# Hedgehog attention and a gated causal convolution on one core: the first loads in another order, with a new list of steps

## The chip, the core and the metric

The kernel runs on one core of a Trainium2 chip. The core has five engines that run side by side, each through its own queue and in the order of that queue: PE (TensorE, matrix products), DVE (VectorE), ACT (ScalarE), POOL (GpSimd) and SP (SyncE). The last only starts transfers here and passes on semaphores. Transfers between the chip's memory and the core run on 16 DMA engines. They can be started from SP's queue, from ACT's queue and from POOL's queue. A transfer that changes the type on its way (float32 in memory, bfloat16 on the core) is started from POOL.

The metric is the device time of one execution in microseconds (us). The kernel before took 229.55 us (median of 3 runs, 228.45 to 229.55).

## The reference

There are 8 batches with 8 heads, 576 positions and head size 64. `q`, `k` and `v` come as float32. What is computed, cut to what matters:

```python
def phi(x):                                   # w_phi: 64 x 128
    proj = x @ w_phi
    proj = proj - max(abs(proj), axis=-1)
    return concatenate([exp(proj), exp(-proj)])
q_p, k_p = phi(q), phi(k)
kv = einsum('bhsf,bhsd->bhfd', k_p, v)
z = sum(k_p, axis=2)
num = einsum('bhsf,bhfd->bhsd', q_p, kv)
den = einsum('bhsf,bhf->bhs', q_p, z) + 1e-06
x = num / den                                 # to (batch, 576, 512)

gate = sigmoid(causal depthwise convolution of x with 5 taps)
out = (gate * (x @ w_val)) @ w_out
```

## The kernel before, in words

**Tiling.** The work is cut into 32 units, four for each batch. A unit is a pair of heads (`hp`, 0 to 3). Positions are split into 9 planes of 64. Planes 0 to 7 of a pair of heads make the unit itself. The ninth plane of all eight heads of a batch is gathered into one more piece per batch, whose steps carry an `e` at the end of the name. When the four units and the piece of a batch are through, the batch goes through convolution, `w_val` and `w_out`; the ninth planes of two batches share one last piece of that.

**The list of steps.** Everything after a short preamble is written out by hand in the string `ORDER`. A token such as `PQA3@0` is one step: its name, the unit or batch, after `@` the PSUM banks, after `:` the engine (A for ACT, D for DVE, P for POOL). A loop at the end of the kernel goes through the tokens inside `tc.manual_schedule()` and calls `op_<name>`. So each engine's queue holds its instructions in the order of the list, and no scheduler moves them. The steps that the texts below speak of:

- `LKa`, `LKb`, `LQa`, `LQb`: load heads 2 and 3, or heads 4 to 7, of batch 0's K or Q (`LKa0` is the second pair of heads, 128x576; `LKb0` the third and fourth, 128x2x576). `LK`, `LQ`, `LV`: all four pairs of a later batch. `LE`: the ninth plane of V. `LWV`, `LWO`: the two weights. All of these are started from POOL (line 288 for K and Q, 286 for V, 291 for `LE`, 321 and 330 for the weights). `LVa0` and `LVb0` load batch 0's V in float32 from SP, in two transfers each (line 286).
- The first pair of heads of batch 0 comes in float32 through two buffers named `QT` (line 195); `CK0` on DVE and `CQ0` on ACT turn it into bfloat16.
- `T`: eight transposes on PE, K first, then Q (line 344). `Tc`: the copy of the result out of PSUM. `PK`, `PQA`: projections of K and of Q (line 357). `mKa`, `mKb`, `mQ`: the row maxima on DVE (line 374). `Ka`, `Kb`: the exponentials of K on ACT, two instructions each (line 438). `E`: exponentials of the maxima (line 423).
- `DMQ`: on POOL, the maxima of Q spread over a diagonal, tile `DM` (line 409). `PQa`, `PQb`: the projection of Q in the other layout (line 527). `SH`: two products that subtract the maxima and read `DM` (line 543). `Qp`, `Qm`: the exponentials of Q on ACT (line 557).
- `V`: on POOL, V times the exponentials `E` (line 463, then a small cast). `DG0`: on POOL, the diagonal matrices of the convolution. `KV`, `KVM`, `NUM`, `RCP`, `XN`, `XP`, `XC`: the rest of the attention. `HL`, `GA`, `TH`, `VA`, `GV`, `OUT`, `OE`, `ST`: the convolution, the gate, `w_val`, `w_out` and the stores from SP (line 875).
- `FL`: a product of zeros on PE that nobody reads (line 253). There are 16 of them in the list, and 8 more in the preamble (line 226).

**Semaphores of the loads.** The loads that POOL starts signal their end through eight semaphores, `DMASW0` to `DMASW7`, which the program uses in turn. The ninth load uses the first one's semaphore again, and for that POOL waits, before it starts the ninth, until the first has landed; the tenth waits for the second, and so on.

**The preamble before.** It stands outside the hand-written order:

```python
    for name, eng in (("k", nc.sync), ("q", nc.scalar)):
        ...
        eng.dma_start(first[name], src[name][0, :, 0, :])
    wtmp = const.tile([P, F], FP32, name="wtmp")
    nc.sync.dma_start(wtmp[0:D, :], w_phi[:, :])
    nc.scalar.dma_start(wtmp[D:P, :], w_phi[:, :])
```

In the built program ACT starts the half of `w_phi` first and Q after it.

Of the kernel before, what the change touches and what calls it, by code (L numbers as in the profile page):

```python
# [33 lines left out]
WQ4 PQb4 SH4 Qm4 Qp4 Tc3:D PQA3@0 Tc5:D mKa2 LWV0 LV1 FL2@3 Ve0:P FL12@3 KV0@7 DMQ2:P DMQe0:P LE1 E2 FL7@3
PK3@3,2 KVM0:A Ka3 mQ3 DMQ3:P mKb3 KV1@4 KVM1:D mKa3 V2:P NUM0@0 Kb3 RCP0 FL15@4 XN0 T7@6 E3 Tc7:D WC0:A WC1:A
PQa2@4 WQ2 PQb2 SH2 PQa3@0 PQA5@2 WQ3 Qp2 mQ5 PQb3 XP0@6 T6@7 Tc6:D SH3 LWO0 NUM1@2 RCP1 XN1 Qm2 V3:P LQ2
XC0:D Qp3 KV2@4 PQea0@2 WQe0 PK5@5,7 mKb5 PQeb0 SHe0 Qm3 PQA6@0 mQ6 FL6@6 KVM2:A Qe0 V4:P KV3@4 NUM2@2 XP1@6
KVM3:D RCP2 XN2 Ka5 FL5@0 XC1:A Kb5 NUM3@0 WC2:A mKa5 NUMe0@3 WC3:A E5 XP2@6 PK6@4,2 RCPe0 XNe0 XPe0@3 Ve1:P
KV4@7 KVM4:A RCP3 XN3 XP3@5 PQa5@0 WQ5 XCe0:D XC2:D NUM4@6 XC3:D LWO1 mKa6 DMQ5:P RCP4 XN4 PQb5 HL0:P Kb6 SH5
VA0_0@3 Ka6 Qm5 Qp5 GA0@6,4 mKb6 V5:P KV5@2 KVM5:D T9@0 NUM5@1 Tc9:D THy0 PK7@4,5 RCP5 LWO2 E6 THx0 VA0_2@0  # L40
XN5 LV2 XP4@1 Ka7 XC4:A GV0_0 DMQe1:P PQa6@6 DMQ6:P GV0_2 mKa7 Kb7 T8@2 Tc8:D mKb7 WQ6 PQb6 PQea1@0 WQe1 SH6
Qm6 Qp6 V6:P LWO3 E7 PQeb1 PQA7@3 mQ7 SHe1 Qe1 LE2 VA0_1@2 GV0_1 KV6@5 KVM6:D PK8@7,6 mKa8 Te2@3 Kb8 DMQ7:P
# [942 lines left out]
```

## Time and profile before

| | before |
|---|---|
| median of the runs | 229.55 us |
| the profiled execution's own time | 229.49 us |
| its span, from the first to the last recorded instruction | 227.6 us |
| mean granted TensorE clock | 0.974 of full speed |
| busy: PE, DVE, ACT, POOL | 206.7, 187.1, 195.8, 164.1 us |
| waits of POOL for ACT's `E` (step `V`), for DVE's maxima (step `DMQ`) | 13.9 us, 11.9 us |

The profile is one execution. Its own time is 1.9 us above its span, which is what lies outside the recorded instructions. Busy times of matmuls include modelled ends, so a PE that is busy all the time is not PE at its peak. In rows of the timeline the first number is the start, the second the time covered, both in us; a bracket at the end gives the idle time of the engine before the row and what ended it. In rows of transfers the last number is the median time from the start of the issue to the landing. Where a row stands for several instructions that run into each other, the time is that of all.

### The profile page before, as it was taken

The page shows a single profiled execution, that of the slowest core. Times are in us where ns is not written, and L with a number is a line of the kernel's source. Part 1 is how long each engine was busy: PE and PEld are TensorE (multiplying, and loading weights), DVE is VectorE, ACT ScalarE, POOL GpSimd, SP SyncE. Part 2 cuts the span into 40 slices and gives each one's busy share as a digit, 9 for nine tenths or more (in the row PEclk, how much of TensorE's full clock was granted, in tenths as well). Part 3 has the DMA queues.
Part 4 walks back from the last instruction along what each step waited for, and adds up shares of the span by engine and source line. Part 5 has one row for each costly group of instructions (what it writes and reads, how often), then busy time and mean ns, then how long its engine had stood idle before and what let it go on. Part 6 is the DMA issues. An engine that isn't in the chain of part 4 may idle for free.

```text
span 227.6 us, 9113 instructions
## 1 busy us (share of the span) xinstructions
PE 206.7 (91%) x3884; PEld 135.6 (60%) x3884; DVE 187.1 (82%) x336; ACT 195.8 (86%) x389; POOL 164.1 (72%) x199
## 2 busy tenths in 40 slices
...
ACT  4439899999999989999999999999999999985350
POOL 7339999799989967994979874989983595851000
...
GB/s 139 212 180 105 209 136 45 114 39 115 70 143 107 167 240 95 16 177 128 119 116 97 127 96 68 128 170 189 176 106 3 6 80 111 95 49 3 141 131 145
DMA packets 27842, 26.12 MB, mean 115 GB/s; under 512 B 5653, under 2 KB 22933, under 8 KB 27802
## 3 DMA queue, kind: packets, MB, share of 16 engines
...
## 4 chain that ended last, share of the span: by engine, by line
PE 62%; DVE 15%; ACT 13%; issue 4%; DMA 3%; POOL 1%; ACTq 0%; DVEq 0%; POOLq 0%
PE PS L811 11%; PE PS L840 10%; PE PS L357 6%; ACT KT L438 5%; PE PS L575 5%; PE PS L485 5%; PE PS L776 5%; PE PS L344 4%; ACT QT L557 4%; DVE XN L595 3%; PE PS L527 3%; DMA QT<-in_q_dram 3%; DVE MK L374 2%; DVE MQ L374 2%; PE PS L605 2%
## 5 line engine op out<-in xcount | busy, mean ns | idle before, releaser
L438 ACT ACTIVATE KT<-PS 128x512 bf16<-128x512 f32 x128 | 68.7, 623 | 5.8 <-PE PS L357 4.7
L463 POOL TENSOR_TENSOR VT<-vN,E 128x1024 bf16<-128x1024 bf16 x28 | 53.3, 1905 | 15.0 <-ACT E L423 13.9
L557 ACT ACTIVATE QT<-PS 128x1024 bf16<-128x1024 f32 x64 | 63.1, 1054 | 0.8 <-PE PS L543 0.6
L374 DVE TENSOR_REDUCE MK<-PS 128x4 f32<-128x512 f32 x64 | 43.0, 683 | 2.1 <-PE PS L357 1.8
L374 DVE TENSOR_REDUCE MQ<-PS 128x8 bf16<-128x1024 f32 x32 | 39.0, 1220 | 6.8 <-PE PS L357 6.0
L409 POOL TENSOR_TENSOR DM<-id,MQ 128x512 bf16<-128x512 bf16 x32 | 33.3, 1039 | 12.5 <-DVE MQ L374 11.9
L840 PE MATMUL PS<-WOUT,GV 128*128 128x512 bf16 x128 | 32.2, 380 | 1.4 <-issue 1.4
L811 PE MATMUL PS<-XT,WVAL 128*128 128x512 bf16 x128 | 31.8, 380 | 0.1
L357 PE MATMUL PS<-W,T 64*128 64x128 bf16 x512 | 25.1, 221 | 5.5 <-ACT KTe L678 2.2
L357 PEld LDWEIGHTS <-T 64*128 64x128 bf16 x512 | 17.7, 96 | 13.2 <-issue 5.8
L485 PE MATMUL PS<-VT,KT 128*128 128x65 bf16 x512 | 24.5, 194 | 0.6 <-ACT QT L557 0.5
L485 PEld LDWEIGHTS <-KT 128*128 128x128 bf16 x512 | 21.8, 98 | 4.0 <-issue 0.8
L832 DVE SCALAR_TENSOR_TENSOR GV<-GATE,PS 128x512 bf16<-128x512 bf16 x32 | 20.9, 681 | 3.2 <-ACT GATE L800 1.6
L595 DVE TENSOR_TENSOR XN<-PS,RCP 128x512 bf16<-128x512 f32 x32 | 22.1, 692 | 1.3 <-DVE RCP L590 0.2
L150 DVE COPY T<-PS 128x1024 bf16<-128x1024 bf16 x29 | 19.6, 683 | 2.7 <-PE PS L344 2.6
L575 PEld LDWEIGHTS <-QT 128*128 128x128 bf16 x512 | 18.6, 97 | 4.9 <-issue 1.3
L489 PE MATMUL PS<-VZ,KTe 128*128 128x65 bf16 x128 | 21.3, 192 | 0.0
L575 PE MATMUL PS<-KVS,QT 128*128 128x65 bf16 x512 | 20.8, 193 | 0.3
L463 POOL TENSOR_TENSOR VZ<-vE,Ee 64x512 bf16<-64x512 bf16 x16 | 16.7, 1042 | 4.3 <-ACT Ee L423 3.7
L800 ACT ACTIVATE GATE<-PS 128x1024 bf16<-128x1024 f32 x16 | 15.8, 1037 | 3.7 <-PE PS L776 3.7
L527 PE MATMUL PS<-T,W 64*128 64x256 bf16 x128 | 18.6, 284 | 0.3
L840 PEld LDWEIGHTS <-GV 128*128 128x128 bf16 x128 | 11.0, 97 | 12.5 <-issue 2.3
...
## 6 DMA issues: line engine op xcount, KB each, us to landing
out_dram<-OS SPq DMA_DIRECT2D x28, 256.0 KB, 3.3
qN<-in_q_dram POOLq DMA_DIRECT2D x7, 576.0 KB, 6.1
kN<-in_k_dram POOLq DMA_DIRECT2D x7, 576.0 KB, 7.4
vN<-in_v_dram POOLq DMA_DIRECT2D x14, 256.0 KB, 6.4
OS<-in_v_dram SPq DMA_DIRECT2D x4, 256.0 KB, 7.7
...
```

The lines of the kernel that those rows point to most:

```text
L357: (nc.tensor.matmul(PS[:, banks[g], jj * F:(jj + 1) * F], T[row(g), n, jj, :, :].rearrange("p a t -> p (a t)"), W2[row(g), :], start=True, ...
L374: nc.vector.tensor_reduce(dst, x, AX.X, ALU.max, apply_absolute_value=True)
L409: engines[eng].tensor_tensor(u.DM[:, :, :], id64[:, :].unsqueeze(1).to_broadcast([P, n, 64]), u.MQ[:, :, :].rearrange("p j g -> p (j g)"). ...
L438: nc.scalar.activation(u.KT[:, ft, par, :, :].rearrange("p b f -> p (b f)"), PS[:, u.PK[par], :], AF.Exp, scale=1.0 if ft == 0 else -1.0,)
L463: engines[eng].tensor_tensor(dst[:, :, :, 0:D], x.unsqueeze(1).to_broadcast([rows, 2, n, D]), e.unsqueeze(3).to_broadcast([rows, 2, n, D]) ...
L485: nc.tensor.matmul(o, u.KT[:, ft, y % 2, h2 * 2 + y // 2, :], u.VT[:, ft, h2 * 4 + y, :], start=(y == 0), stop=False,)
L527: return nc.tensor.matmul(PS[:, u.PQ + a, :].rearrange("p (j g t) -> p g j t", g=2, t=64)[:, g, :, :], W2[row(g), :], u.T[row(g), 1, :, a, :],
L557: nc.scalar.activation(u.QT[:, ft, :, :, :].rearrange("p a n t -> p a (n t)"), half(u.PQ, 512), AF.Exp, scale=1.0 if ft == 0 else -1.0,)
L575: (nc.tensor.matmul(u.NUM[:, jj // 2, x * E1:(x + 1) * E1], u.QT[:, ft, jj // 2, 4 * h2 + 2 * (jj % 2):4 * h2 + 2 * (jj % 2) + 2, :].rearr ...
L595: nc.vector.tensor_tensor(u.XN[:, :, :, :], numview(u)[:, :, :, 0:D], u.RCP[:, :, :].unsqueeze(3).to_broadcast([P, 2, 4, D]), ALU.mult,)
L811: nc.tensor.matmul(PS[:, m.val[r], :], WVAL[:, dt, r, :], xt(b)[:, dt, 4:12, :].rearrange("p n t -> p (n t)"), start=(dt == 0), stop=(dt = ...
L840: nc.tensor.matmul(PS[:, m.out[j], :], m.GV[:, r, j * P:(j + 1) * P], WOUT[:, r, :], start=(r == 0), stop=(r == 3),)
```

## The change

**The preamble.** The first five transfers are now written inside `tc.manual_schedule()`. Their order on each queue is the written one: SP starts K, the first half of `w_phi` and the taps, as before; ACT now starts Q first and the second half of `w_phi` after it.

**The list.** `ORDER` is a new list with the same 1241 steps. All loads of batch 0's K and Q (`LQa0`, `LKa0`, `LQb0`, `LKb0`) stand ahead of batch 1's (`LQ1`, `LK1`). Both halves of batch 0's V stand ahead of the first `WQ` in SP's queue, where only `LVa0` did. Units now go 0, 1, 2, 3, 4 where they went 0, 1, 4, 2, 3. Steps change engines here and there: `HL` on ACT twice more (6 instead of 8 on POOL), `Tc` on ACT 5 instead of 3, `XC` on ACT 6 instead of 11, `XCe` on ACT 3 instead of 1, `Tce` on ACT none instead of one, `WC` on ACT 2 and POOL 2 instead of ACT 4, `KVM` on ACT 14 instead of 15, `OE` on ACT 20 instead of 19, `ND0` on POOL instead of DVE. The diff, with the list cut to its first two lines:

```diff
 ORDER = """
-ZV1:D ZV0:A IF0:D CK0 ZV2:D CQ0 T0@1 LKa0 LQ1 Tc0:A TP0@6 CW0 W0 PQA0@3 PK0@5,1 LQa0 FL8@0 FL1@7 FL11@6 LK1
-ND0:D mQ0 DG0:P FL10@0 Ka0 FL4@6 PQa0@6 mKb0 mKa0 E0 T1@2 FL3@0 Tc1:D PQA1@3 mQ1 PK1@0,5 T4@2 Kb1 Tc4:D mKb1
...
+LQa0 IF0:D ZV1:D CK0 ZV0:A CQ0 TP0@4 LKa0 T0@1 CW0 W0 T1@0 Tc0:D PK0@4,5 ZV2:D mKa0 PQA0@6 Tc1:A PK1@3,2
+FL12@1 LQb0 Kb0 mQ0 Ka0 PQA1@0 LKb0 LQ1 mKb1 mKb0 ND0:P Ka1 T2@6 Tc2:D E0 LK1 LE0 mQ1 LVa0 FL0@7 Te0@5 Tce0:D
...
     first = {}
-    for name, eng in (("k", nc.sync), ("q", nc.scalar)):
+    for name in ("k", "q"):
         t = featq.tile([P, 2, 2, 8, 64], BF16, name="QT")
         t = t[:, :, :, :, :].rearrange("p f h n t -> p (f h n t)").bitcast(FP32)
         first[name] = t[:, 0:NPL * D]
-        eng.dma_start(first[name], src[name][0, :, 0, :])
     wtmp = const.tile([P, F], FP32, name="wtmp")
-    nc.sync.dma_start(wtmp[0:D, :], w_phi[:, :])
-    nc.scalar.dma_start(wtmp[D:P, :], w_phi[:, :])
     cw5 = const.tile([5, DM], FP32, name="cw5")
-    nc.sync.dma_start(cw5[:, :], moe_conv_w[:, :])
+    with tc.manual_schedule():
+        nc.sync.dma_start(first["k"], src["k"][0, :, 0, :])
+        nc.scalar.dma_start(first["q"], src["q"][0, :, 0, :])
+        nc.sync.dma_start(wtmp[0:D, :], w_phi[:, :])
+        nc.scalar.dma_start(wtmp[D:P, :], w_phi[:, :])
+        nc.sync.dma_start(cw5[:, :], moe_conv_w[:, :])
```

The first place is POOL's queue in the opening, from the load of batch 1's Q on. Rows with `DMA` are loads; `kN`, `qN` and `vN` are the loaded K, Q and V, `GV` the buffer in which `w_val` lands, `WOUT` that of `w_out`, `DM` the spread maxima; the bracket names the semaphores that the instruction waits for. Before:

```order
L288 DMA qN<-in_q_dram 128x4x576
L288 DMA qN<-in_q_dram 128x576
L288 DMA kN<-in_k_dram 128x4x576
L270 TENSOR_TENSOR id_128<-ident 128x32 [waits Pool_49]
L271 TENSOR_TENSOR id_128<-id_128,ident 128x32 [waits Pool_49]
L272 TENSOR_TENSOR id_128<-id_128,ident 128x32 [waits Pool_49]
L273 TENSOR_TENSOR DIAG<-id_128,cwT 128x640 [waits DVE_49,Pool_49]
L288 DMA kN<-in_k_dram 128x2x576
L409 TENSOR_TENSOR DM<-id_126,MQ 128x512 [waits DVE_49]
```

And the change:

```order
L289 DMA qN<-in_q_dram 128x4x576
L251 TENSOR_TENSOR id_129<-ident 128x64 [waits Pool_49]
L289 DMA kN<-in_k_dram 128x4x576
L292 DMA vE<-in_v_dram 128x4x64 x2
L322 DMA GV<-in_moe_w_val_dram 128x4x512 [waits DMASW0_49]
L289 DMA qN<-in_q_dram 128x4x576 [waits DMASW1_49]
L287 DMA vN<-in_v_dram 64x8x256 [waits DMASW2_49]
L287 DMA vN<-in_v_dram 64x8x256 [waits DMASW3_49]
L289 DMA kN<-in_k_dram 128x4x576 [waits DMASW4_49]
L331 DMA WOUT<-in_moe_w_out_dram 32x4x512 [waits DMASW5_49]
L410 TENSOR_TENSOR DM<-id_129,MQ 128x512 [waits DVE_49,Pool_49]
```

Before, five loads were started ahead of the first `DM`, and the ninth load of POOL came 10 rows behind it. Now fourteen are started ahead of it (four more stand above the rows shown), and the last six wait for the first six: `DMASW4` is that of `LQ1`, `DMASW5` that of `LK1`. The three small sums of `DG0` have moved behind the second `DM`.

The second place is ACT's queue from the first conversion of Q (`qN<-QT`) to the first exponentials of Q (`QT<-PS`). `KT<-PS` are exponentials of K, two rows for a step, `KTe` those of the ninth planes. Before:

```order
L244 ACTIVATE qN<-QT 128x576
L148 ACTIVATE T<-PS 128x1024
L438 ACTIVATE KT<-PS 128x512 x2
L423 ACTIVATE E<-MK 128x8 x2
L438 ACTIVATE KT<-PS 128x512 x8
L557 ACTIVATE QT<-PS 128x1024
```

And the change:

```order
L245 ACTIVATE qN<-QT 128x576
L147 ACTIVATE T<-PS 128x1024
L439 ACTIVATE KT<-PS 128x512 x6
L424 ACTIVATE E<-MK 128x8 x2
L439 ACTIVATE KT<-PS 128x512 x4
L679 ACTIVATE KTe<-PS 128x512 x2
L439 ACTIVATE KT<-PS 128x512 x2
L558 ACTIVATE QT<-PS 128x1024 x2
```

Six steps of K (12 rows) and the ninth planes of K of batch 0 now stand ahead of the first exponential of Q, where five steps of K did.

More of the change, by code (lines that the diff above doesn't have):

```diff
@@ L28 @@
 ORDER = """
-ZV1:D ZV0:A IF0:D CK0 ZV2:D CQ0 T0@1 LKa0 LQ1 Tc0:A TP0@6 CW0 W0 PQA0@3 PK0@5,1 LQa0 FL8@0 FL1@7 FL11@6 LK1
-ND0:D mQ0 DG0:P FL10@0 Ka0 FL4@6 PQa0@6 mKb0 mKa0 E0 T1@2 FL3@0 Tc1:D PQA1@3 mQ1 PK1@0,5 T4@2 Kb1 Tc4:D mKb1
-LKb0 LVa0 PQA4@2 Kb0 Ka1 mQ4 PK4@4,5 Kb4 DMQ0:P LE0 WQ0 DMQ1:P PQb0 SH0 Qm0 LQb0 mKa1 Ka4 Te1@1 Tce1:D mKb4
-LK2 DMQ4:P PQa1@2 PKe1@0 mKe1 E1 WQ1 PQb1 SH1 Qp0 LVb0 FL13@5 FL0@5 FL9@5 Ee1 Qp1 V0:P FL14@5 Te0@5 mKa4 mQe1
-T2@6 Qm1 E4 KTe1 V1:P Tce0:D PKe0@4 Tc2:D mKe0 Ee0 PQA2@0 mQe0 mQ2 T3@3 T5@6 KTe0 PK2@2,7 Ka2 mKb2 Kb2 PQa4@4
@@ L34 @@
[L34 to L42, printed above, removed]
-XP5@2 XC5:D NUM6@4 RCP6 VA0_3@0 PQa7@1 WQ7 XN6 Tce2:A mKb8 Ka8 XP6@4 XC6:D E8 GV0_3 PQb7 SH7 PK9@6,3 Qp7 Qm7
@@ L99 @@
-OE7_0:A ST7_1 ST7_3 ST7_0
+LQa0 IF0:D ZV1:D CK0 ZV0:A CQ0 TP0@4 LKa0 T0@1 CW0 W0 T1@0 Tc0:D PK0@4,5 ZV2:D mKa0 PQA0@6 Tc1:A PK1@3,2
+FL12@1 LQb0 Kb0 mQ0 Ka0 PQA1@0 LKb0 LQ1 mKb1 mKb0 ND0:P Ka1 T2@6 Tc2:D E0 LK1 LE0 mQ1 LVa0 FL0@7 Te0@5 Tce0:D
+mKa1 LE1 Kb1 PK2@7,6 T3@4 Ka2 Tc3:D PKe0@0 mKa2 FL10@5 PQA2@2 mQ2 LVb0 LWV0 KTe0 PQa0@4 WQ0 LQ2 LV1 Kb2 PQb0
+LK2 LWO3 DMQ0:P SH0 FL4@7 mKb2 FL15@7 FL9@7 DMQ1:P DG0:P mKe0 PQa1@2 FL3@7 FL14@7 WQ1 PQb1 SH1 Qm0 Qp0 Ee0 Qp1
+T4@7 LWO1 DMQ2:P mQe0 DMQe0:P Qm1 Tc4:D Te1@6 Ve0:P FL5@4 Tce1:D PQA4@4 mQ4 PKe1@0 PQA3@6 mQ3 E1 PK4@2,3 E2
```

120 lines of the change are left out of this document (65 added, 55 removed).

## The prediction, on record before the change was run

> **What bounds the kernel now.** The page comes first, its busy times and its slices, then the busy times by stretch.
>
> ```profile
> PE 206.7 (91%) x3884; PEld 135.6 (60%) x3884; DVE 187.1 (82%) x336; ACT 195.8 (86%) x389; POOL 164.1 (72%) x199
> ACT  4439899999999989999999999999999999985350
> POOL 7339999799989967994979874989983595851000
> ```
>
> ```profile
> 0.00:10.00 10.00, 5.05 (x28) 2.51 (x30) 3.79 (x13) 4.26 (x5) 4.84 (x14) 0.88 0.83 166
> 10.00:20.00 10.00, 8.35 (x84) 4.22 (x80) 7.48 (x10) 5.70 (x13) 6.39 (x8) 0.67 0.88 142
> 20.00:30.00 10.00, 6.78 (x95) 3.95 (x94) 8.51 (x14) 9.35 (x23) 9.84 (x13) 0.94 1.18 202
> 30.00:40.00 10.00, 8.85 (x182) 6.75 (x179) 8.77 (x15) 10.00 (x21) 9.96 (x13) 1.00 0.66 76
> 60.00:80.00 20.00, 19.94 (x438) 13.05 (x438) 18.92 (x33) 19.35 (x38) 18.55 (x23) 1.00 0.92 141
> ```
>
> The columns of the second fence are the length, then busy PE, PEld, DVE, ACT and POOL, the granted clock, the DMA share and GB/s. From 60 to 80 us PE, ACT and DVE are all busy for 95% or more: no engine has room to win back lost time. What can be won or lost lies in the opening, where ACT is busy for 4.26 and 5.70 of 10 us, and in the tail. From 20 to 40 us POOL has nothing to spare either (9.84 and 9.96 of 10). So I follow ACT, and POOL when it feeds ACT. The timeline of ACT in the opening:
>
> ```profile
> 7.21 0.68 ACT L244 ACTIVATE qN<-QT 128x576 bf16<-128x576 f32 x1 [2.68 <-DMA QT<-in_q_dram]
> 8.59 1.02 ACT L148 ACTIVATE T<-PS 128x1024 bf16<-128x1024 bf16 x1 [0.70 <-PE PS L344]
> 10.74 1.08 ACT L438 ACTIVATE KT<-PS 128x512 bf16<-128x512 f32 x2 [1.12 <-PE PS L357]
> 12.78 0.31 ACT L423 ACTIVATE E<-MK 128x8 f32<-128x8 f32 x2 [0.95 <-DVE MK L374]
> 15.70 4.03 ACT L438 ACTIVATE KT<-PS 128x512 bf16<-128x512 f32 x8 [2.61 <-PE PS L357]
> 19.56 1.08 ACT L557 ACTIVATE QT<-PS 128x1024 bf16<-128x1024 f32 x1
> 21.62 1.09 ACT L557 ACTIVATE QT<-PS 128x1024 bf16<-128x1024 f32 x1
> 24.72 1.17 ACT L678 ACTIVATE KTe<-PS 128x512 bf16<-128x512 f32 x2
> 27.70 2.07 ACT L438 ACTIVATE KT<-PS 128x512 bf16<-128x512 f32 x4 [0.65 <-PE PS L357]
> ```
>
> ACT waits 2.68 us for Q, later 2.61 us for the second unit, whose inputs land late. From 15.70 us on it has one more gap, 0.65 us.
>
> **When the loads land.** The answers on the DMA issues, one by one, and the issues' own starts on POOL:
>
> ```profile
> kN<-in_k_dram POOLq DMA_DIRECT2D x1, 144.0 KB, 5.7
> qN<-in_q_dram POOLq DMA_DIRECT2D x1, 144.0 KB, 9.9
> kN<-in_k_dram POOLq DMA_DIRECT2D x1, 576.0 KB, 12.3
> kN<-in_k_dram POOLq DMA_DIRECT2D x1, 288.0 KB, 6.8
> OS<-in_v_dram SPq DMA_DIRECT2D x1, 256.0 KB, 9.7
> ```
>
> ```profile
> 1.28 0.75 POOL L288 DMA_DIRECT2D kN<-in_k_dram  x1 [0.34 <-issue]
> 2.36 1.33 POOL L288 DMA_DIRECT2D qN<-in_q_dram  x2
> 3.67 0.83 POOL L288 DMA_DIRECT2D kN<-in_k_dram  x1
> 10.64 0.76 POOL L288 DMA_DIRECT2D kN<-in_k_dram  x1
> ```
>
> POOL's loads land in the order of their issue: `LKa0` (144 KB) at 1.28 + 5.7 = 7.0 us; `LQ1` and `LQa0` (720 KB more) by about 3.1 + 9.9 = 13.0; `LK1` (576) at 3.67 + 12.3 = 16.0; `LKb0` (288) at 10.64 + 6.8 = 17.4. That is 720 KB in 6.0 us, 120 KB/us, up to 13.0, and 864 KB in 4.4 us, 196 KB/us, after it. The difference is what SP and ACT move meanwhile: the last of the first V pair lands at about 3 + 9.7 = 12.7 us, by when K, Q, the small ones and V make some 1160 KB, about 99 KB/us from 1 us on.
>
> **The change, part by part.** *Q first.* Q would be in by 4.5 to 6.5 us instead of 7.2; `ZV0` holds ACT until 4.5. But on PE unit 1's transposes now stand ahead of unit 0's projections, and they wait for `LKa0`, now second in POOL's queue: 7.0 + 144/120 = 8.2 us. So Q first costs nothing and wins nothing by itself; PE goes on at 8.2 us either way.
>
> *Batch 0 ahead of batch 1.* `LKb0` now ends 864 KB of POOL's queue, which by the row of `LQa0` is 13.0 us, where `LQb0` was issued only at 17.78 us. ACT's steps ahead of the first exponential of Q are six of K (four took 15.70 to 19.56, 0.97 each), E (0.31), KTe (0.98 up to the next row) and one copy (1.02). Started at about 9 us and held up for about 1 us by the third unit, they end at about 18.1 us. Taken alone, this part is a gain.
>
> *The wait on POOL.* `DMQ0`, which the first exponential of Q needs, now stands behind fourteen loads, and the fourteenth, `LWO3`, waits for `DMASW5`, that is until `LK1` has landed. Issuing alone would not hurt: fourteen at about 0.75 us from 1.28 us on end near 12.7. The landing does. Ahead of and with `LK1` stand 144+144+288+288+576+576 = 2016 KB. SP now has both halves of V at the start, 512 KB more, so at 99 KB/us its traffic lasts until 12.7 + 5.2 = 17.9 us. With 144 KB in at 7.0 and 120 KB/us until 17.9, 1452 KB are in; the other 564 at 196 take 2.9: `LK1` lands at 20.8 us. Bounds: 196 KB/us throughout gives 16.6, 120 throughout 22.6. I take 20.8, since both rates come from the same rows under the same kind of traffic.
>
> The Trainium skill, DMA: Bandwidth & Descriptors, section "Anatomy of one DMA — SWDGE (gpsimd) path", puts a transfer from this queue at about 2.0 us plus its bytes over 436 GB/s; as an estimate from that page all of the opening's traffic, about 3.8 MB, would be in near 12 us and `DMQ0` would wait for no load. The 12.3 us of the 576 KB row above disagree.
>
> Behind the wait, POOL runs `LWO3`, then `DMQ0`; PE adds `SH0`:
>
> ```profile
> 34.46 0.59 POOL L330 DMA_DIRECT2D WOUT<-in_moe_w_out_dram  x1
> 11.64 1.03 POOL L409 TENSOR_TENSOR DM<-id,MQ 128x512 bf16<-128x512 bf16 x1 [0.24 <-DVE MQ L374]
> 18.48 0.71 PE L543 MATMUL PS<-DM,minus 64*128 64x512 bf16 x2
> 10.64 2.31 PE L253 MATMUL PS<-zero 128*128 128x512 bf16 x5
> 8.00:12.00 4.00, 3.40 (x28) 2.10 (x29) 2.09 (x5) 2.11 (x3) 2.32 (x3) 0.50 1.18 238
> ```
>
> 20.8 + 0.59 + 1.03 + about 0.4 (the two products overlap) = 22.8 us for the first exponential of Q. By then ACT has done 1.02 + 5.8 + 0.31 + 0.98 = 8.1 us of work that counts; before, it had done that at 21.4 us (1.02 + 1.08 + 0.31 by 13.1, the remaining 5.7 from 15.70). **Term one: 22.8 - 21.4 = +1.4 us**, bounds 16.6 giving -2.8 (18.6 against 21.4) and 22.6 giving +3.2. Queued behind `DMQ0` on POOL are `DMQ1`, `DG0`, `DMQ2` and all of V; behind `SH0` on PE stand five fillers, unit 1's Q and then batch 1's first transposes. DVE and ACT wait for these.
>
> *After the wait.* PE will have stood still from about 16 us on. The last row shows what follows such a stand: after PE's idle time from 4.7 to 7.9 us the clock is 0.50, and five fillers take 2.31 us. Between `SH0` and `SH1` are five fillers and unit 1's products of Q, about 3.5 us cold; ACT has 2.0 us to do meanwhile (`Qm0`, `Qp0`, `Ee0`). That is 1.5 us lost cold and nothing warm; I take 1.0, nearer cold. On the other side, the gap of 0.65 us at 27.05 goes. **Term two: +0.35.** The first V is due on POOL at about 32.5 us instead of 22.2, since `Ve0` now stands ahead of it; batch 0's last V ends at about 41 us. Its product `KV3` ran at 39.8 us before and stands later in the new list, so I cost this at nothing more; if that cover is gone it is up to 1 us.
>
> *Steps on other engines.* By means of the page's groups: ACT gains two `HL` of about 1.0 (the POOL copy of that shape takes 1.02), two `Tc` of 1.05, one `OE` of 0.62 and two `XCe` of 0.45, and loses five `XC` of 0.61, two `WC` of 0.68, one `Tce` of 0.67 and one `KVM` of 0.43: **+0.2 us**. DVE comes to about the same (+0.1), PE does the same work.
>
> *The tail.*
>
> ```profile
> 217.51 3.71 PE L840 MATMUL PS<-WOUT,GV 128*128 128x512 bf16 x16
> 219.15 1.08 ACT L860 ACTIVATE OS<-PS 128x512 f32<-128x512 f32 x2 [1.70 <-PE PS L840]
> 219.78 4.95 SPq L875 DMA_DIRECT2D out_dram<-OS  x8
> ```
>
> The eight last stores run back to back from the first finished piece. Before, that piece is done after 6 of the last 16 products, now after 4, by the order of the `OUT7` steps: 2 x 0.22 = 0.43 earlier. **-0.4 us**, bounds -0.43 and 0, if the stores then wait for the last piece.
>
> **Sum** against the profiled execution's 229.49 us (span 227.6 and 1.9 outside; the median of the runs is 229.55): 229.49 + 1.4 + 0.35 + 0.2 - 0.4 = **231.0 us**. The new list's body from 45 us on is taken as neutral; before, the body has about 7 us of idle ACT between 40 and 200 us, so it could be a microsecond or two either way.
>
> **The rivals.** *The loads come sooner.* If `LK1` lands by 16.6 us, `SH0` no longer holds ACT, and the earlier inputs count in full: 229.49 - 2.8 - 0.65 + 0.2 - 0.4 = 225.8 us. For it: 196 KB/us was reached when POOL's queue was alone. Against it: SP moves 512 KB more at that very time. It decides once `LK1` lands before about 18. This is also where the page's rule would lead. Chance 0.20.
>
> *The loss is won back.* The first exponential of Q is late, but DVE and PE are not behind by as much (DVE has unit 3's copy and batch 0's ninth planes done by then), and the body's idle ACT takes it up: 229.49 + 0.2 - 0.4 = 229.3 us. For it: POOL waits 13.9 us for E over the run, so it can catch up. Against it: ACT's 19.35 of 20 us. Chance 0.22.
>
> *Slower still.* The 120 KB/us hold all the way, `LK1` lands at 22.6, PE stays cold for all five fillers, and V's delay reaches `KV3`: 231.0 + 1.8 + 0.5 + 0.7 = 234.0 us. It decides from a landing after about 22 us. Chance 0.12.
>
> *The preamble does nothing.* Q may land no sooner, since K and Q now start together on the same engines. With PE waiting for `LKa0` until 8.2 us, a Q at 6.5 changes no number above; it has no time of its own.
>
> **How the numbers follow.** The forecast, a late `DMQ0` at 231.0 us, own range 229.8 to 233.0, has 0.46. Half a per cent, 1.15 us around 229.55, is about what a measurement of this kernel can tell from no change: 228.40 to 230.70. Above it lies about 0.29 of the forecast's chance, the slower rival's 0.12 and 0.05 of the loss won back: slower 0.46. Within it lie the forecast's other 0.16 and 0.13: 0.29. Below it the first rival and 0.04: faster 0.25 with rounding. The range from 226.3 to 234.0 us leaves out about a tenth on each side at most. Cases of both signs hold most of the chance, so the forecast's own range stands beside it.
>
> **What would show it.** In the changed profile: POOL's row of `LWO3` starts when `LK1` lands, at 20 to 22 us, with no busy POOL between the issue of `LE1` and it but five loads; the first `DM` follows it; ACT's first QT row starts at 22 to 23.5 us with an idle time of 3 to 5 us put down to PE L544; the granted clock is near 0.5 to 0.7 from 16 to 26 us; the third unit's transposes come near 13 us, ahead of 22.8 before. I am wrong in the cause if `DM` stands at 12 to 18 us, and wrong in its worth if ACT is that late and the time is still at or below 229.

## The result, and the profile after

The changed kernel took 226.86 us (median of 7 runs, 225.52 to 227.71) beside 229.55 us for the kernel before (7 runs): a ratio of 0.988, 95% interval 0.984 to 0.991, some 2.8 us faster. The forecast was 231.0 us and slower; the time lies below its own range of 229.8 to 233.0 us, near the low end of the wide one (226.3 to 234.0). Taken again beside other kernels it came to 227.09 us, ratio 0.988 (0.984 to 0.993).

The profiled execution after took 225.52 us, span 223.6, the lowest of its runs. First the page: the engines' totals, and the slices of ACT and of the granted clock.

```profile
PE 202.7 (91%) x3848; PEld 134.1 (60%) x3884; DVE 186.1 (83%) x337; ACT 195.8 (88%) x387; POOL 163.7 (73%) x200
ACT  5591899999999999998999999999999999887640
PEclk9995899999999999999999999999999999999998
```

ACT's busy time is the same 195.8 us in a span 4.0 us shorter. The hole that the prediction spoke of is there: ACT has a slice with 1, and the granted clock is 5 in that slice and 8 in the next. The timeline of POOL after, where the wait stands:

```profile
16.28 0.76 POOL L289 DMA_DIRECT2D kN<-in_k_dram  x1 [3.76 <-DMA qN<-in_q_dram]
19.22 0.55 POOL L331 DMA_DIRECT2D WOUT<-in_moe_w_out_dram  x1 [2.18 <-DVE MQe L375]
19.79 2.04 POOL L410 TENSOR_TENSOR DM<-id,MQ 128x512 bf16<-128x512 bf16 x2
28.68 1.90 POOL L464 TENSOR_TENSOR VT<-OS,E 128x1024 bf16<-128x1024 f32 x1
```

`LK2` starts when `LQ1` has landed (16.3 us), `LWO3` when `LK1` has (19.2), and the first `DM` right behind it. The releaser that the second row names is an inference and wrong: the row's wait is for `LK1`'s semaphore by the order of the program. The last row is the first `V`. What ACT and PE make of it:

```profile
4.60 0.68 ACT L245 ACTIVATE qN<-QT 128x576 bf16<-128x576 f32 x1 [0.28 <-DMA QT<-in_q_dram]
8.14 1.02 ACT L147 ACTIVATE T<-PS 128x1024 bf16<-128x1024 bf16 x1 [2.85 <-PE PS L345]
21.54 1.94 ACT L558 ACTIVATE QT<-PS 128x1024 bf16<-128x1024 f32 x2 [4.57 <-PE PS L544]
24.67 1.94 ACT L558 ACTIVATE QT<-PS 128x1024 bf16<-128x1024 f32 x2 [1.00 <-PE PS L544]
```

```profile
20.89 0.61 PE L544 MATMUL PS<-DM,minus 64*128 64x512 bf16 x2 [4.60 <-POOL DM L410]
```

PE stands for 4.60 us and ACT for 4.57, then ACT once more for 1.00: the late `DMQ0` is as forecast. The second profile of the same kernel had it later still, close to the forecast's figures (`LWO3` was put at 20.8, the first exponential of Q at 22.8). POOL, then ACT, of that execution:

```profile
20.56 0.55 POOL L331 DMA_DIRECT2D WOUT<-in_moe_w_out_dram  x1 [2.04 <-DMA kN<-in_k_dram]
```

```profile
22.88 1.94 ACT L558 ACTIVATE QT<-PS 128x1024 bf16<-128x1024 f32 x2 [4.21 <-PE PS L544]
```

So the wait came as said and the time did not. The busy times by stretch from 95 us on say where to look. Columns: length, then busy PE, PEld, DVE, ACT, POOL, clock, DMA share, GB/s. Before:

```profile
95.00:160.00 65.00, 64.15 (x1276) 43.49 (x1277) 60.61 (x107) 62.45 (x126) 52.93 (x62) 1.00 0.75 126
160.00:210.00 50.00, 49.70 (x1048) 33.66 (x1045) 44.33 (x83) 46.43 (x92) 32.12 (x36) 1.00 0.34 69
```

And after (the page's first line shows that 36 of its matmul records are missing, so PE's own busy time reads a little low here):

```profile
95.00:160.00 65.00, 63.83 (x1257) 43.41 (x1263) 61.95 (x108) 62.32 (x127) 55.38 (x66) 1.00 0.70 112
160.00:210.00 50.00, 49.08 (x1076) 33.46 (x1085) 40.66 (x77) 45.76 (x88) 26.80 (x29) 1.00 0.39 95
```

In the 65 us from 95 on DVE does 1.3 us more and POOL 2.5 us more than before, and 3.7 and 5.3 us less is left for the next stretch (a part of it is steps that changed engines). So the body has moved too. The experiments put a price on the opening and on the body.

### The profile page after: what moved, and what is told of

The parts are those of the page before. It is cut to its first block, busy times and chain, and to the rows that moved or that the text cites. A ratio compares the mean times of both kernels' runs of the same rounds, so it can differ in the third digit from the quotient of the medians.

```text
span 223.6 us, 9071 instructions
## 1 busy us (share of the span) xinstructions
PE 202.7 (91%) x3848; PEld 134.1 (60%) x3884; DVE 186.1 (83%) x337; ACT 195.8 (88%) x387; POOL 163.7 (73%) x200
## 4 chain that ended last, share of the span: by engine, by line
PE 69%; DVE 9%; POOL 8%; DMA 5%; issue 5%; ACT 1%; POOLq 0%; DVEq 0%; SPq 0%; ACTq 0%
PE PS L841 12%; PE PS L812 10%; PE PS L486 7%; PE PS L576 6%; PE PS L358 6%; DMA qN<-in_q_dram 5%; PE PS L345 5%; PE PS L528 4%; PE PS L777 4%; PE PS L606 3%; PE PS L544 3%; DVE MQ L375 2%; POOL DM L410 2%; DVE GV L833 2%; POOL VT L464 2%
## 5 line engine op out<-in xcount | busy, mean ns | idle before, releaser
L841 PE MATMUL PS<-WOUT,GV 128*128 128x512 bf16 x112 | 30.6, 380 | 1.3 <-DVE GV L833 0.3
L812 PE MATMUL PS<-XT,WVAL 128*128 128x512 bf16 x114 | 30.2, 380 | 1.2 <-issue 0.3
L149 DVE COPY T<-PS 128x1024 bf16<-128x1024 bf16 x27 | 18.5, 685 | 8.5 <-PE PS L345 8.1
L833 DVE SCALAR_TENSOR_TENSOR GV<-GATE,PS 128x512 bf16<-128x512 bf16 x32 | 21.4, 682 | 3.7 <-ACT GATE L801 2.4
L812 PEld LDWEIGHTS <-WVAL 128*128 128x128 bf16 x128 | 11.0, 97 | 10.9 <-issue 0.5
```

Of the source, the lines that this page charges most:

```text
L812: nc.tensor.matmul(PS[:, m.val[r], :], WVAL[:, dt, r, :], xt(b)[:, dt, 4:12, :].rearrange("p n t -> p (n t)"), start=(dt == 0), stop=(dt = ...
L833: nc.vector.scalar_tensor_tensor(out=m.GV[:, r, :], in0=m.GATE[:, r, :], scalar=1.0, in1=PS[:, m.val[r], :], op0=ALU.add, op1=ALU.mult,)
L841: nc.tensor.matmul(PS[:, m.out[j], :], m.GV[:, r, j * P:(j + 1) * P], WOUT[:, r, :], start=(r == 0), stop=(r == 3),)
```

## The experiments

All times are medians; the ratio is to the kernel before, run beside each, with its 95% interval. Sums over kernels that didn't run side by side are made from the ratios, a hundredth being 2.3 us.

| kernel | us | ratio |
|---|---|---|
| changed kernel; again | 226.86; 227.09 | 0.988 (0.984 to 0.991); 0.988 (0.984 to 0.993) |
| old list, new preamble | 229.01 | 0.999 (0.997 to 1.002) |
| new list, old preamble | 227.67 | 0.992 (0.989 to 0.995) |
| old to 45 us, new after | 233.45 | 1.018 (1.015 to 1.022) |
| new to 45 us, old after | 235.49 | 1.026 (1.024 to 1.029) |
| new to 95 us, old after | 229.01 | 0.997 (0.994 to 1.000) |
| new to 160 us, old after | 227.52 | 0.990 (0.986 to 0.994) |
| old to 95 us, new after | 230.44 | 1.003 (1.000 to 1.006) |
| new, three loads behind `DM`; again | 221.02; 221.64 | 0.963 (0.959 to 0.966); 0.964 (0.960 to 0.968) |
| new, only `LWO3` behind | 224.65 | 0.977 (0.973 to 0.982) |
| three loads behind, old list from 95 us | 223.94 | 0.975 (0.971 to 0.978) |
| three loads behind, eight fillers less | 223.47 | 0.971 (0.967 to 0.976) |
| new order, old engines | 249.50 | 1.086 (1.080 to 1.092) |
| old list, eight fillers less | 228.78 | 0.996 (0.992 to 0.999) |

A total mixes what a change wins with what its place in the list costs. One more measure separates them. Every step has a fixed number of weight loads on PE, and the traces have all of these, so one can count off when PE starts its 129th step, say (fillers aside). After 128, 151, 222 and 386 steps of PE both lists have given it exactly the same steps; after 48 steps they differ in one. The times below that name such a step are counted from the traces; they stand in no view as a row.

### The preamble alone

The old list with the new preamble, and the new list with the old one (the two parts of the change apart; no line is edited besides):

```diff
     with tc.manual_schedule():
         nc.sync.dma_start(first["k"], src["k"][0, :, 0, :])
         nc.scalar.dma_start(first["q"], src["q"][0, :, 0, :])
...
-LQa0 IF0:D ZV1:D CK0 ZV0:A CQ0 TP0@4 LKa0 T0@1 CW0 W0 T1@0 Tc0:D PK0@4,5 ZV2:D mKa0 PQA0@6 Tc1:A PK1@3,2
+ZV1:D ZV0:A IF0:D CK0 ZV2:D CQ0 T0@1 LKa0 LQ1 Tc0:A TP0@6 CW0 W0 PQA0@3 PK0@5,1 LQa0 FL8@0 FL1@7 FL11@6 LK1
...
```

> The list of before with the preamble of the change alone (Q started ahead of the second half of w_phi). Preamble theory (Q first by itself brings the gain): Q lands at about 4.6 us instead of 7.2, time 227 us, ratio 0.989. Body and opening theory: Q lands as early, but unit 1 still waits for its Q plane until about 13 us, so 229.3 to 229.9 us, ratio 0.998 to 1.002.

> The list of the change with the preamble of before. Preamble theory: the gain is gone, 229.5 us. Body and opening theory: unit 0 starts some 1 to 2.5 us later, but the first exponential of Q waits for POOL's DM until 21.5 us all the same, so 226.5 to 227.3 us, ratio 0.987 to 0.990.

In the old list Q came 2.3 us sooner and the time stayed. In the new list the old preamble cost 0.4% (0.9 us), but the intervals overlap. ACT's timeline of the new list with the old preamble:

```profile
7.14 0.68 ACT L239 ACTIVATE qN<-QT 128x576 bf16<-128x576 f32 x1 [2.61 <-DMA QT<-in_q_dram]
9.38 1.02 ACT L143 ACTIVATE T<-PS 128x1024 bf16<-128x1024 bf16 x1 [1.55 <-PE PS L339]
22.41 1.94 ACT L552 ACTIVATE QT<-PS 128x1024 bf16<-128x1024 f32 x2 [2.91 <-PE PS L538]
```

The first copy of transposes runs at 9.38 us, where the changed kernel's first profile has it at 8.14 and its second at 9.82. The forecast had PE waiting for `LKa0` until 8.2 us whatever Q does. `LKa0` landed at 2.34 + 5.7 = 8.0 us in this run and at 2.34 + 4.7 = 7.0 and 2.33 + 6.4 = 8.7 in the two profiles of the changed kernel, and the copies follow these landings. That Q first is worth anything by itself isn't shown.

### The lists cut at 45 us

The first attempt to tell opening from body: one list up to its `HL0`, the other for what is left, PSUM banks given anew where they clash.

```diff
 ORDER = """
-(the new list's steps up to HL0)
+(the old list's steps up to HL0)
 (the new list's other steps)
```

> The preamble and list of before up to and with step HL0 of batch 0 (the first 220 steps, about 45 us), then every remaining step in the order of the changed list; 8 steps get another PSUM bank where the old one would be taken. Body theory (the gain lies in the order of the steps behind batch 0, the opening is worth nothing): 226.5 to 227.5 us, ratio 0.986 to 0.992. Opening theory (the gain lies in the loads and the first 45 us): 229 to 230 us, ratio 0.997 or more.

> The preamble and list of the change up to and with step HL0 of batch 0 (212 steps), then every remaining step in the order of the list before; one step gets another PSUM bank. Body theory: 229 to 230 us, ratio 0.997 or more. Opening theory: 226.5 to 227.5 us, ratio 0.986 to 0.992. If both halves bring a part, both hybrids lie near 228.

Both are slower than either whole list, which no theory had. PE's rows at the seams, first of the old opening with the new body, then of the other:

```profile
47.55 1.02 PE L808 MATMUL PS<-XT,WVAL 128*128 128x512 bf16 x4 [2.64 <-ACT KT L435]
```

```profile
46.31 0.29 PE L482 MATMUL PS<-VT,KT 128*128 128x65 bf16 x4 [2.14 <-POOL VT L464]
```

The two lists differ in 18 steps at that place, and the seam makes PE wait, more than these two rows show: PE starts its 129th step at 82.6 and 80.4 us, where the whole lists have 74.6 to 76.2. Behind that step the first run needs 149.2 us to the end, as the changed kernel does (149.1 and 149.2), and the second 152.1, about as the old list does (151.7, with the new preamble 151.5). So the totals say nothing of either half, and the traces say that the body behind that step is worth 2.3 to 2.9 us. A better place was sought for the next lists: at 95 us the lists differ in six steps, at 160 us in two stores.

### The lists cut at 95 and at 160 us

```diff
 ORDER = """
-(the old list)
+(the new list's first 468, or 966, steps)
+(the old list's other steps, in its order)
```

> The list of steps is the new one for its first 468 steps (to about 95 us) and the old one for the rest, with the new preamble; the two lists differ there in six steps only, so the seam should cost nothing. The whole old list with the new preamble takes 229.0 us, the whole new one 226.9. Theory 'the gain is spread over the body' (PE's lead of after over before is 0.6 us at 45 us, 2.3 at 90, 3.0 at 150, 4.1 at 210, so some six tenths of it is won by 95): 227.8 us. Theory 'PE's halt of 1.4 us in an OUT step at 82.9 us and the opening are all of it': 226.9. Theory 'the gain lies at the end': 229.0.

> The new list for its first 966 steps (to about 160 us), the old one for the rest, new preamble; the lists differ there by two stores. Theory 'spread over the body': 227.3 us, as eight tenths of the lead are won by then. Theory 'halt and opening': 226.9. Theory 'the end': 229.0, if the last 60 us are what differs.

> The old list for its first 464 steps (to about 95 us), the new one for the rest, new preamble: the complement of the run above that changes at the same place. Theory 'spread over the body': 228.1 us, the later four tenths of the gain. Theory 'halt and opening': 229.0, with PE's halt near 82.9 us again. Theory 'the end': 226.9.

Going from the old list to the new one by stretches, with the new preamble throughout: 0.9994 (all old), 0.9967 (new to 95 us), 0.9899 (new to 160), 0.9876 (all new). By these totals the first 95 us are worth 0.6 us, the next 65 us 1.6 and the rest 0.5, each with an uncertainty of about 1 us. These cuts have small seams too. PE's row at the cut at 95 us, and at the one at 160:

```profile
88.30 0.65 PE L572 MATMUL PS<-KVS,QT 128*128 128x65 bf16 x16 [0.65 <-DVE XN L592]
```

```profile
172.30 0.40 PE L572 MATMUL PS<-KVS,QT 128*128 128x65 bf16 x8 [0.84 <-DVE GV L829]
```

A pause of this size isn't in the whole lists there. If each costs its length, the first 95 us are worth 0.65 us more than said and the last stretch 0.8 less, that is about nothing, with the tail in it.

PE's steps give the price without the seams. Lengths in us, from two profiles each:

| PE's steps | old list: before; with the new preamble | new list: the changed kernel's two profiles |
|---|---|---|
| up to the 128th | 75.9; 75.7 | 74.6; 76.0 |
| 129th to 151st | 12.2; 12.0 | 11.0; 11.0 |
| 152nd to 222nd | 31.7; 31.7 | 31.5; 31.6 |
| 223rd to 386th | 76.3; 76.3 | 74.9; 74.9 |
| 387th to the end | 31.5; 31.5 | 31.7; 31.7 |

The opening differs from one execution to the next; the other lengths come back. The second row holds the halt of the old list (below). The fourth is the cleanest: it is 76.27 to 76.37 us in every run that has the whole stretch from the old list, behind the new opening too (76.28 in the run with the new list to 95 us), and 74.93 to 74.96 in every run that has it from the new one with its own engines, behind the old opening too (74.93 in the third run of this section). So these 1.3 us belong to the list, whatever ran ahead. Of them, 0.4 us is less idle time of PE (0.8 us before, 0.5 after). The other 1.0 us lies in four convolutions (`GA3` to `GA6`), each with 80 products of one form: from the first start to the last they take 1.44, 1.17, 1.25 and 1.46 us in the old list and 1.18, 0.98, 0.99 and 1.15 in the new one. `GA6` before and after (the second number holds the last product's 0.37 us besides):

```profile
194.31 1.84 PE L776 MATMUL PS<-XT,DIAG 32*32 32x512 bf16 x80
```

```profile
190.48 1.53 PE L777 MATMUL PS<-XT,DIAG 32*32 32x512 bf16 x80
```

Banks and neighbours of these steps differ between the lists; which of them makes the same products slower stays open.

The third run, the complement, came to 230.44 where the sums give 227.3 (0.9994 - 0.0091). Its PE rows show why:

```profile
82.78 0.59 PE L837 MATMUL PS<-WOUT,GV 128*128 128x512 bf16 x2 [1.12 <-issue]
89.62 0.38 PE L354 MATMUL PS<-W,T 64*128 64x128 bf16 x7 [0.61 <-DVE XN L592]
93.96 1.02 PE L837 MATMUL PS<-WOUT,GV 128*128 128x512 bf16 x4 [1.20 <-DVE MQ L371]
```

The first is the halt of the old list (below); the other two, 1.8 us, are a seam at which PE waits for DVE. The 152nd to the 222nd step take 34.6 us here and 31.5 to 31.7 in the whole lists, so the seam costs 3 us, all of the excess. It is too dear for this run's total to price anything. The run with the new list to 95 us has a seam there as well, of 0.8 us (32.5). Its busy times in the middle stretch are the old list's:

```profile
95.00:160.00 65.00, 64.16 (x1278) 43.50 (x1275) 60.57 (x107) 62.43 (x126) 52.90 (x62) 1.00 0.75 127
```

DVE 60.57 and POOL 52.90, as in the old list (60.61, 52.93), against 61.95 and 55.38 in the changed kernel, whose first 95 us are the same as this run's.

### The wait on POOL

Three steps of the new list moved, so that `DMQ0`, `DMQ1` and `DG0` no longer stand behind the loads that wait for `LQ1` and `LK1`:

```diff
 mKa1 LE1 Kb1 PK2@7,6 T3@4 Ka2 Tc3:D PKe0@0 mKa2 FL10@5 PQA2@2 mQ2 LVb0 LWV0 KTe0 PQa0@4 WQ0 LQ2 LV1 Kb2 PQb0
-LK2 LWO3 DMQ0:P SH0 FL4@7 mKb2 FL15@7 FL9@7 DMQ1:P DG0:P mKe0 PQa1@2 FL3@7 FL14@7 WQ1 PQb1 SH1 Qm0 Qp0 Ee0 Qp1
-T4@7 LWO1 DMQ2:P mQe0 DMQe0:P Qm1 Tc4:D Te1@6 Ve0:P
+DMQ0:P SH0 FL4@7 mKb2 FL15@7 FL9@7 DMQ1:P DG0:P LK2 mKe0 PQa1@2 FL3@7 FL14@7 WQ1 PQb1 SH1 Qm0 Qp0 Ee0 Qp1
+T4@7 DMQ2:P mQe0 DMQe0:P Qm1 Tc4:D Te1@6 Ve0:P LWO3 LWO1
```

> The changed kernel, with three steps of the list moved: LK2 behind DG0, LWO3 and LWO1 behind Ve0. DMQ0, DMQ1 and DG0 then stand ahead of the loads that wait for LQ1 and LK1 on POOL. Both theories: the first QT row of ACT starts near 17 us in place of 21.5, and ACT's idle time ahead of it falls from 4.57 us to under 1. Theory 'the wait on POOL costs its length': the end comes as much earlier, 226.9 - 4 = 222.5 to 224 us. Theory 'the opening has slack that the wait uses up' (PE and ACT have their work by the same inputs, which land no earlier): the steps behind it wait for the landings instead, the lead at 45 us is under 1 us and the time is 226 to 227.5 us.

221.02 us, 3.7% under the kernel before and 5.8 us under the changed one: past the lower end of what the first theory expected, and the best version of the study. POOL's timeline of it, then ACT's:

```profile
13.15 1.05 POOL L406 TENSOR_TENSOR DM<-id,MQ 128x512 bf16<-128x512 bf16 x1
18.35 0.82 POOL L285 DMA_DIRECT2D kN<-in_k_dram  x1
23.18 1.13 POOL L327 DMA_DIRECT2D WOUT<-in_moe_w_out_dram  x2
24.37 1.90 POOL L460 TENSOR_TENSOR VT<-OS,E 128x1024 bf16<-128x1024 f32 x1
```

```profile
16.08 1.08 ACT L675 ACTIVATE KTe<-PS 128x512 bf16<-128x512 f32 x2 [0.18 <-PE PS L643]
18.00 1.98 ACT L554 ACTIVATE QT<-PS 128x1024 bf16<-128x1024 f32 x2
```

`DM` runs at 13.15 instead of 19.79 us, ACT goes from K to Q without a gap, and the loads start when nothing waits for them. PE starts its 49th step at 33.8 us, where the new opening with the wait has 38.1 to 39.7, and needs 185.6 us from there to the end, as the changed kernel does: the whole gain lies in the opening. A smaller step, `LWO3` alone behind `Ve0` (`LK2` and `LWO1` as in the changed kernel):

```diff
-LK2 LWO3 DMQ0:P SH0 FL4@7 mKb2 FL15@7 FL9@7 DMQ1:P DG0:P mKe0 PQa1@2 FL3@7 FL14@7 WQ1 PQb1 SH1 Qm0 Qp0 Ee0 Qp1
-T4@7 LWO1 DMQ2:P mQe0 DMQe0:P Qm1 Tc4:D Te1@6 Ve0:P
+LK2 DMQ0:P SH0 FL4@7 mKb2 FL15@7 FL9@7 DMQ1:P DG0:P mKe0 PQa1@2 FL3@7 FL14@7 WQ1 PQb1 SH1 Qm0 Qp0 Ee0 Qp1
+T4@7 LWO1 DMQ2:P mQe0 DMQe0:P Qm1 Tc4:D Te1@6 Ve0:P LWO3
```

> The changed kernel with one step moved: LWO3 behind Ve0. DMQ0 then waits on POOL only for LK2, which waits for the landing of LQ1 (16.0 us), and no longer for LK1's (19.0). DM starts near 17.1 us instead of 19.8, and ACT's first QT row near 18.9 instead of 21.5. Theory 'the wait costs its length': two thirds or more of what the three moves won, 226.9 - 2.7 to - 5 = 222 to 224 us. Theory 'the three moved loads cost by their own traffic, not by the wait': LK2 still runs ahead, so less than half: 224 to 226.9 us.

224.65 us: 2.2 us of the 5.8, less than the first theory had and within what the second had, by which the three loads cost by their traffic. PE's timeline of this run, then POOL's:

```profile
19.26 0.39 PE L540 MATMUL PS<-DM,minus 64*128 64x512 bf16 x2 [1.16 <-POOL DM L406]
29.67 0.29 PE L482 MATMUL PS<-VT,KT 128*128 128x65 bf16 x4 [1.67 <-POOL VT L464]
```

```profile
17.38 0.76 POOL L285 DMA_DIRECT2D kN<-in_k_dram  x1 [3.54 <-DVE T L145]
22.33 0.59 POOL L327 DMA_DIRECT2D WOUT<-in_moe_w_out_dram  x1
```

The wait for `DM` is down from 4.60 to 1.16 us, but PE now waits 1.67 us for the first `V`. What is left of the wait is `LK2`, still ahead of `DMQ0`: POOL stands for 3.54 us until `LQ1` has landed (again the named releaser is not the one that the order gives). `LWO1`, now the fourteenth load, costs its 0.59 us and waits for nothing. `DM` runs at 18.16 us, where it ran at 13.15 with all three moved, and the first `V` at 27.52, where it ran at 28.68 in the changed kernel and at 24.37 with all three moved. So the wait has two prices: for `DM` at once, and for everything behind it on POOL. PE's stand has a third: from 16 to 26 us the mean granted clock is 0.66 in the changed kernel and 1.00 with the three loads moved. That is why it cost more than its own 4.6 us. The rows name POOL and no load where PE waits; no run moved the loads' traffic without the wait, so a share of it in the 5.8 us is not excluded.

Last, whether wait and body are two things, and both kernels again on one chip. The list with the three steps moved for its first 468 steps, and the old list from there:

```diff
 ORDER = """
-(the new list)
+(the new list's first 468 steps, with LK2, LWO3 and LWO1 moved as above)
+(the old list's other steps, in its order)
```

> The kernel with LK2, LWO3 and LWO1 moved for its first 468 steps (to about 90 us), the old list for the rest. Theory 'the wait on POOL and the order of the body from 95 us on are two costs apart': 229.0 (the same with the late DM) - 5.8 = 223.2 us, within 0.8; that is 2.2 us over the new list to the end. Theory 'the new body gains only where it makes up for the late opening': 221.0 to 221.8 us, no dearer than the new body.

> The changed kernel as it is, beside the others on one chip: 226.9 us as before, within 0.5. If it comes to 228 or more, the gain of the change is half of what it was put at.

> The kernel with LK2, LWO3 and LWO1 moved, again: 221.0 us within 0.5, so 5.4 to 6.3 us under the changed kernel of the same job.

223.94, 227.09 and 221.64 us. The wait costs 5.5 us here (0.9884 - 0.9644 = 2.4%); the new list from 95 us on is worth 2.3 us with the early `DM` and was worth 2.1 with the late one (0.9967 - 0.9876). They are two costs apart: behind the early `DM`, too, the 223rd to the 386th step take 76.28 us with the old list and 74.94 with the new. Of the 2.1 and 2.3 us, 0.8 is the seam of the mixed lists.

### The engines of the steps

The new list's order, with each step from `HL0` on put on the engine it has in the old list:

```diff
-HL0:A
+HL0:P
...
-XC4:D
+XC4:A
...
-OE0_3:A
+OE0_3:D
...
```

> The changed kernel with the order of the new list, but from HL0 on each step on the engine that it has in the old list (42 steps change engines, nearly all between ACT and DVE). Theory 'the body is won by which engine has which step': 228 to 229 us, the gain of 2.3 us mostly gone. Theory 'it is won by the order of PE's steps, PE being busy without a gap': 226.9 within 0.8, the 0.2 us of ACT's work that the prediction counted being lost in it.

249.50 us, 22.5 us worse than the changed kernel; neither theory was near. PE's timeline and POOL's:

```profile
48.30 1.13 PE L773 MATMUL PS<-XT,DIAG 32*32 32x512 bf16 x64 [2.44 <-POOL XT L145]
```

```profile
44.64 1.92 POOL L460 TENSOR_TENSOR VT<-vN,E 128x1024 bf16<-128x1024 bf16 x1
47.21 1.04 POOL L145 COPY XT<-XT 128x1008 bf16<-128x1008 bf16 x1
```

The changed kernel has this `HL0` on ACT at 43.33 us. On POOL it stands behind a `V` and comes at 47.21, and the convolution on PE waits. This is only the first such wait: PE starts its 129th step at 87.4 us, against 74.6 and 76.0 in the changed kernel, and loses as much again behind it. The order and the engines are one design; the run doesn't price them apart. What it refutes is the prediction's way of costing these moves by busy time alone (+0.2 us).

### The halt in an OUT step, and the fillers

Before, PE stood for 1.36 us in the middle of a step and waited for nothing that the profile shows. The row of the kernel before:

```profile
84.22 0.59 PE L840 MATMUL PS<-WOUT,GV 128*128 128x512 bf16 x2 [1.36 <-issue]
```

It stood in the same step, `OUT1_3`, ahead of its last two products, in every run with the old list there (1.12 to 1.23 us in the others; the shortest is shown above) and in no run that had the new list with its own engines there. In the new order with the old engines there is one of 0.88 us, in the step `SH11`. Eight fillers, products of zeros that nobody reads, were taken out of the old list ahead of it:

```diff
-FL9@5
-FL14@5
...
-FL6@6
-FL5@0
```

> The kernel before without the last eight of its sixteen fillers (dummy products on zeros that feed nothing, 22 to 40 us), which takes some 16 instructions out of PE's stream ahead of 40 us. PE's halt of 1.2 to 1.4 us at 82.9 us stood in the same step, OUT1_3, in every run of the old list, after the same number of PE's instructions. Theory 'the halt belongs to a place in PE's stream, where its instructions come late': it moves some 16 instructions on, into another step behind OUT1_3, or is hidden; the time is 229.5, or 228.2 if it is hidden. Theory 'it belongs to what OUT1_3 reads or writes': it stays in OUT1_3.

228.78 us, 0.4% (0.1 to 0.8) under the kernel before. PE's timeline:

```profile
79.66 1.91 PE L834 MATMUL PS<-WOUT,GV 128*128 128x512 bf16 x8
81.62 0.31 PE L351 MATMUL PS<-W,T 64*128 64x128 bf16 x4
82.45 0.29 PE L351 MATMUL PS<-W,T 64*128 64x128 bf16 x4 [0.52 <-issue]
```

The eight products of the two `OUT1` steps now run through. The halt has moved on into the next projection of K, again in the middle of a step, and is 0.52 us long. It belongs to a place in PE's stream of instructions, not to the step: in all six kernels, this one and the one with the old engines included, it comes after exactly 1246 products of PE. The gain of 1.0 us doesn't price it, since fewer fillers change the opening too. In this profile, the fastest of the ten runs at 226.98 us, 1.7 us are won by PE's 49th step and 0.8 where the halt is.

The same eight-filler cut on the kernel with the three loads behind `DM` (the eight fillers behind `SH1`) went the other way:

```diff
-FL5@4
-FL6@4
...
-FL13@5
-FL2@6
```

> The kernel with LK2, LWO3 and LWO1 moved, and besides without the eight fillers (dummy products on zeros that feed nothing) that stand behind SH1 in the list. Theory 'PE sets the end from 25 us on': 8 x 0.22 = up to 1.8 us less than the 221.0 us of the kernel with the fillers, 219.2 to 220.5. Theory 'ACT sets it there': the same 221.0 within 0.5.

223.47 us, about 2 us slower than with the fillers (221.02 and 221.64; the intervals of the ratios are 0.966 to 0.976 against 0.959 to 0.968). Neither theory allowed a loss. The busy times by stretch, first with the fillers and then without:

```profile
28.00:32.00 4.00, 3.90 (x78) 2.58 (x74) 3.84 (x7) 4.00 (x11) 4.00 (x5) 1.00 0.91 152
```

```profile
24.00:28.00 4.00, 1.76 (x23) 0.96 (x23) 4.00 (x7) 4.00 (x8) 3.94 (x7) 0.99 1.36 200
28.00:32.00 4.00, 3.88 (x63) 3.44 (x63) 2.69 (x6) 3.41 (x10) 4.00 (x5) 0.58 1.00 168
```

With PE idle for more than half of 24 to 28 us, the granted clock from 28 to 32 is 0.58 instead of 1.00. The fillers pay for themselves there: the Trainium skill, TensorE: Matmul & The Clock Gate, section "HAM oscillation — how this bites in real kernels", warns of idle gaps of PE over about 3.4 us, and here 2.2 us of idle time in 4, in pieces of at most 1.25 us, were enough. And in the tail a halt turned up that no other run has, in the middle of the 80 products of a convolution:

```profile
208.83 0.85 PE L773 MATMUL PS<-XT,DIAG 32*32 32x512 bf16 x41 [1.18 <-issue]
```

Here a halt comes where there was none with the fillers. This profile is the slowest of its six runs (224.63 us), 3.4 us above the one with the fillers: 2.2 us of that is lost by PE's 49th step, where the clock is low, and 1.5 behind its 386th, where this halt is; 0.3 comes back between.

## Why the prediction was wrong, step by step

**The late `DMQ0`: right.** `LWO3` waits for `LK1`, `DM` follows, ACT stands for 4 to 5 us ahead of the first exponential of Q, then 1.0 us more behind it. The landing of `LK1` was put at 20.8 us; it was 19.2 in one profile and 20.6 in the other (the row below gives 14.0 us from issue to landing for `LK1` and its neighbour), and the first exponential of Q, put at 22.8, came at 21.54 and 22.88. Without the wait the kernel is 5.5 to 5.8 us faster; the rival "the loads come sooner" (225.8) lay 5.2 under the forecast. That rival's cause did not come about: in no profile with the new opening had `LK1` landed by 16.6. The clock came as said as well: 0.66 on the mean from 16 to 26 us. The DMA issues of the changed kernel, for the 576 KB of K:

```profile
kN<-in_k_dram POOLq DMA_DIRECT2D x2, 576.0 KB, 14.0
```

The rule of the Trainium skill, DMA: Bandwidth & Descriptors, section "Anatomy of one DMA — SWDGE (gpsimd) path", that the prediction set against its own rates, would by the estimate made there have had all of it in near 12 us; the 19.2 us disagree.

**The opening's sum: too high by about 1 us.** Terms one and two with the engines made +1.95 us. PE starts its 49th step, at about 39 us, at 38.6 and 38.4 us in two profiles with the old list and at 38.1, 39.6, 39.7 and 39.3 in four with the new opening: three of the four are about 1 us late, and the first profile, where `LK1` landed soonest, is half a microsecond early. The measure of equal work of ACT had the sign right and the size too large. The term for the engines adds up to +0.1 by its own numbers, not to +0.2, and ACT's busy time came out the same. The first `V`, costed at nothing, was put at 32.5 us and started at 28.68; PE's longest wait for V in the changed kernel is 0.33 us, so nothing was about right there, though in the run with `LWO3` alone moved it is 1.67 us.

**The body: this step failed.** "The new list's body from 45 us on is taken as neutral", with a microsecond or two either way. From PE's 49th step to the end of the span the old list takes 189.1 and 188.8 us (before, and with the new preamble) and the new one 185.6 in both profiles of the changed kernel: 3.2 to 3.5 us less. About 0.9 us of it lies between 39 and 76 us, where the late opening is made up again, 1.0 to 1.2 in the next 12 us, where the old list's halt is, 1.3 between PE's 223rd and 386th step, and the last stretch gives 0.2 back. The prediction looked for free room, found ACT busy for 19.35 of 20 us, and concluded that little could move. The room was on PE, the engine that is busy nearly all the time: in a halt of 1.36 us that stands in the profile before, in less idle time, and in products that take longer in one order than in the other. That the halt is gone is luck: the prediction doesn't speak of it. With what the profiles show in place of both steps the sum comes out: 229.49 - 0.5 - 3.5 = 225.5 us for the first profile (225.52) and 229.49 + 1.0 - 3.5 = 227.0 for the second (227.07).

**Q first: right as far as it can be read.** It is worth nothing with the old list (0.999), as said, and with the new one the 0.9 us are not clear of noise. `LKa0`, put at 8.2 us, landed between 7.0 and 8.7.

**Tail: borne out as far as it can be read.** -0.4 was said. The eight last stores start 215.76 - 210.63 = 5.13 us after the start of the last gate's row, where it was 219.78 - 214.16 = 5.62, so 0.5 sooner. The stretch from PE's 387th step to the end takes 0.2 us longer all the same, so the tail as a whole wins nothing. The rows after, on SP and on ACT (before, the gate's row starts at 214.16):

```profile
215.76 4.95 SPq L876 DMA_DIRECT2D out_dram<-OS  x8
```

```profile
210.63 1.94 ACT L801 ACTIVATE GATE<-PS 128x1024 bf16<-128x1024 f32 x2 [1.56 <-PE PS L777]
```

**The rivals.** "The loss is won back" at 229.3 had the right shape, a late exponential of Q and no slower end, but its mechanism, idle time of ACT that takes the loss up, is not what was found: about 1 us was made up by 76 us, but the kernel with the early `DM`, which has no such loss to win back, gains the same there (36.5 us from PE's 49th to its 129th step, 36.5 and 36.4 in the changed kernel, 37.3 in the old list). So the wait cost its full price and more, and the rest of the list paid for it. The prediction named the case itself: wrong in its worth if ACT is that late and the time still at or below 229.
